# First loads in another order, and the statistics of the first chunk in two halves, in a layer norm + S5 + SwiGLU kernel

## The chip, the cores and the metric

The kernel runs on one core of one Trainium2 chip. The metric is the device time of one execution in microseconds; the median of three runs before the change is 200.81 us (200.62 to 201.2).

## The reference

One input x of 2048 tokens by 512 features (bf16) is normalised per token, and three things are added: x itself, a diagonal complex state-space layer (S5) on the normalised input, and a SwiGLU feed-forward block on it with 1792 hidden features.

```python
xn = _layernorm(x, axis=-1)                      # mean and variance over the 512 features
# S5: Bu = xn @ B_bar.T ; h[t] = Lam_bar * h[t-1] + Bu[t] ; y = 2 Re(h @ C.T) + xn * Dskip
# SwiGLU: out = (silu(xn @ w1) * (xn @ w3)) @ w2
return x + S5(xn) + SwiGLU(xn)
```

w1 and w3 are 512 x 1792, w2 is 1792 x 512.

## The kernel before

The 2048 tokens are taken in four blocks of 512; a block has four chunks of 128 tokens, one token to a partition. For each block the kernel normalises the chunks, brings the normalised block to the layout with features on partitions (`xnT`), multiplies it with w1 and w3 for the 14 hidden tiles of 128 (function `glu`), gates the results, projects to the state (`bu`), scans along time, and multiplies gates and states with w2 and C together (`y_fast`). The order of every engine's instructions is the order in which the Python program writes them, since the kernel schedules by hand; side tasks are put between by a small planner (`Filler`), which does not act before the first three hidden tiles are done.

The change touches the start alone, that is block 0 up to its third hidden tile. The names:

- Loads. `nc.sync.dma_start` issues on SP's queue, `nc.scalar.dma_start` on ACT's. Lines 164 to 170 are the first loads. x of block 0 comes by chunk: chunks 0 and 1 in two halves of 256 features each (128 x 256 bf16, 64 KB), one on SP and one on ACT; chunk 3 whole (128 KB) on ACT; chunk 2 whole on SP. Then `load_w` (line 155) loads columns 0 to 255 of w1 (line 156) and of w3 (line 157), and then columns 256 to 511 of both, 256 KB each, all on SP. Both weights bear the name `w_sb` in the profile.
- ACT's program begins with its three loads, then loads a table of functions (line 199). SP's holds loads alone.
- `bulk_loads` (line 172) issues the next stage on SP: columns 512 to 1023 of w1 and w3, block 1 of x, and transposing loads. Its first instruction is a small one on ACT that reads chunk 0's scale and writes into w1, so the loads do not go before that scale is known.
- TensorE begins with ten matmuls on constants (`keep_busy`, line 196).
- `ln_stats` (line 217) takes a chunk's mean and variance on VectorE: one `bn_stats` over 512 features (line 219) and one `bn_aggr` (line 220). `ln_first_rstd` makes the scale on ACT (lines 233 and 234). `ln_apply` (line 224) normalises on VectorE. `ln_first_transpose` transposes on TensorE (line 243) and copies out on ACT (line 244).
- `quarter(cl, fs)` (line 619) are the matmuls of one chunk's 128 tokens with hidden tiles `fs`: the w1 side first, then the w3 side. Tiles 0 and 1 use columns 0 to 255, tile 2 uses columns 256 to 383.
- After the first two quarters come the transposed parameters of S5 (line 315), chunk 2's transposes, tile 2 of chunk 0, chunk 3's transposes, and so on; the dense loop over the other hidden tiles is line 587.

On VectorE the order is: statistics of chunk 0, statistics of chunk 1, chunk 0 normalised in two halves, chunk 1 normalised, statistics of chunks 2 and 3, both normalised.

Of the kernel before, what the change touches and what calls it, by code (L numbers as in the profile page):

```python
# [14 lines left out]
FP32 = DT.float32  # L15
BF16 = DT.bfloat16
FP16 = DT.float16
P = 128
# [45 lines left out]
def kernel(  # L64
# [17 lines left out]
    nc = tc.nc  # L82
    _, S, D = A_x.shape
# [21 lines left out]
    D1, D2 = slice(0, DH), slice(DH, D)  # L105
# [3 lines left out]
    xv = A_x[0].rearrange("(c p) d -> p c d", p=P)  # L109
# [5 lines left out]
    lnp = ctx.enter_context(tc.tile_pool(name="lnp", bufs=2))  # L115
# [28 lines left out]
    mv_all = const.tile([P, NCH, 2], FP32, name="mv_all")  # L144
# [6 lines left out]
    x_blk = [x_all[:, i] for i in range(NBLK)]  # L151
# [3 lines left out]
    def load_w(f0, f1, eng1=nc.sync, eng3=nc.sync):  # L155
        eng1.dma_start(out=w1_sb[:, :, f0:f1], in_=w1v[:, :, f0:f1])
        eng3.dma_start(out=w3_sb[:, :, f0:f1], in_=w3v[:, :, f0:f1])
# [3 lines left out]
        for i in range(0, CPB, n):  # L161
            nc.sync.dma_start(out=x_blk[b][:, i:i + n, :], in_=xv[:, b * CPB + i:b * CPB + i + n, :])

    for c in range(2):
        for eng, dsl in ((nc.sync, slice(0, D // 2)), (nc.scalar, slice(D // 2, D))):
            eng.dma_start(out=x_blk[0][:, c, dsl], in_=xv[:, c, dsl])  # L166
    nc.scalar.dma_start(out=x_blk[0][:, 3, :], in_=xv[:, 3, :])
    nc.sync.dma_start(out=x_blk[0][:, 2, :], in_=xv[:, 2, :])
    load_w(0, 2 * P)
    load_w(2 * P, 4 * P)  # L170

    def bulk_loads():
        nc.scalar.activation(out=w1_sb[:, 0, 4 * P:4 * P + 1], in_=rstd_all[:, 0:1], func=ACT.Copy)
        load_w(4 * P, MID * P)
        load_x(1)
        nc.sync.dma_start_transpose(out=bt[:, 0], in_=A_B_re)
        nc.sync.dma_start_transpose(out=bt[:, 1], in_=A_B_im)
        load_w(MID * P, F)
        nc.sync.dma_start_transpose(out=ct_in[:, :, 0, :], in_=A_C_re)
        nc.sync.dma_start_transpose(out=ct_in[:, :, 1, :], in_=A_C_im)  # L180
# [13 lines left out]
    def keep_busy(n, cols):  # L194
        for _ in range(n):
            nc.tensor.matmul(out=wps[:, 0:cols], lhsT=ones[:, 0:P], rhs=ones[:, 0:cols], start=True, stop=True)
# [20 lines left out]
    def ln_stats(b, cl):  # L217
        stats = lnp.tile([P, 6], FP32, name="stats", bufs=4)
        nc.vector.bn_stats(out=stats, in_=x_blk[b][:, cl, :])
        nc.vector.bn_aggr(out=mv_all[:, b * CPB + cl, :], in_=stats)  # L220

    def ln_apply(b, cl, dsl=slice(0, D)):
        c = b * CPB + cl
        nc.vector.tensor_scalar(out=xn_blk[b][:, cl, dsl], in0=x_blk[b][:, cl, dsl], scalar1=mv_all[:, c, 0:1],
                                scalar2=rstd_all[:, c:c + 1], op0=ALU.subtract, op1=ALU.mult)
# [5 lines left out]
    def ln_first_rstd(cl):  # L231
        lnv = lnp.tile([P, 1], FP32, name="lnv")
        nc.scalar.activation(out=lnv, in_=mv_all[:, cl, 1:2], func=ACT.Ln, bias=eps_t, scale=1.0)
        nc.scalar.activation(out=rstd_all[:, cl:cl + 1], in_=lnv, func=ACT.Exp, scale=-0.5)

    def ln_first_transpose(cl, parts=1):
        n = NDT // parts
        for i in range(0, NDT, n):
            if parts > 1:
                ln_apply(0, cl, slice(i * P, (i + n) * P))  # L240
            pxt = ps_y.tile([P, n, P], BF16, name="y_ps")
            for k in range(n):
                nc.tensor.transpose(out=pxt[:, k, :], in_=xn_blk[0][:, cl, (i + k) * P:(i + k + 1) * P], identity=ident)
            nc.scalar.activation(out=xnT_blk[0][:, i:i + n, cl * P:(cl + 1) * P], in_=pxt, func=ACT.Copy)
# [68 lines left out]
    def params_transpose():  # L313
        pps = ps_y.tile([P, NP3], BF16, name="y_ps")
        nc.tensor.transpose(out=pps, in_=par_rows, identity=ident[0:NP3, 0:NP3])
        return pps

    def params_dt(pps):
        nc.scalar.activation(out=par, in_=pps, func=ACT.Copy)
        nc.scalar.activation(out=dtv, in_=par[:, 0:NPT], func=ACT.Exp)  # L320
        gp.tensor_tensor(out=kr, in0=dtv, in1=lre, op=ALU.mult)

    def params_turn():
        gp.tensor_tensor(out=turn, in0=dtv, in1=lim, op=ALU.mult)
        gp.tensor_scalar(out=turn, in0=turn, scalar1=1.0 / TWO_PI, scalar2=None, op0=ALU.mult)
        gp.tensor_scalar(out=fr, in0=turn, scalar1=MAGIC, scalar2=None, op0=ALU.add)
        gp.tensor_scalar(out=fr, in0=fr, scalar1=-MAGIC, scalar2=None, op0=ALU.add)
        gp.tensor_tensor(out=fr, in0=turn, in1=fr, op=ALU.subtract)
        gp.tensor_scalar(out=t0, in0=turn, scalar1=0.25, scalar2=None, op0=ALU.add)
        gp.tensor_scalar(out=ab, in0=t0, scalar1=MAGIC, scalar2=None, op0=ALU.add)  # L330
        gp.tensor_scalar(out=ab, in0=ab, scalar1=-MAGIC, scalar2=None, op0=ALU.add)
        gp.tensor_tensor(out=ab, in0=t0, in1=ab, op=ALU.subtract)
        gp.tensor_tensor(out=den, in0=lre, in1=lre, op=ALU.mult)
        gp.tensor_tensor(out=t0, in0=lim, in1=lim, op=ALU.mult)
        gp.tensor_tensor(out=den, in0=den, in1=t0, op=ALU.add)
# [245 lines left out]
    def glu(b):  # L581
# [10 lines left out]
        def evac(f, g_ps, u_ps):  # L592
            if f % 2 == 0:
                pair[:] = [glup.tile([P, 2, TBLK], BF16, name="g16"), glup.tile([P, 2, TBLK], BF16, name="u16")]
            g16, u16 = pair
            nc.scalar.activation(out=g16[:, f % 2, :], in_=g_ps, func=ACT.Silu)  # L596
            nc.scalar.activation(out=u16[:, f % 2, :], in_=u_ps, func=ACT.Copy)  # L597
            if f % 2 == 1:
                pend.append((f, g16, u16))

        def gate():
            f, g16, u16 = pend.pop(0)
            bg.own(0.6, -0.5)
            nc.vector.tensor_tensor(out=act_gates(b, f - 1), in0=split(g16), in1=split(u16), op=ALU.mult)  # L604
# [3 lines left out]
        if b == 0:  # L608
            f0 = FIRST
            tiles = first_ps  # L610

            def quarter(cl, fs, parts=1):
                tsl = slice(cl * P, (cl + 1) * P)
                n = NDT // parts
                for side, w in ((0, w1_sb), (1, w3_sb)):
                    for i in range(0, NDT, n):
                        for f in fs:
                            for dt in range(i, i + n):
                                nc.tensor.matmul(out=tiles[2 * f + side][:, tsl], lhsT=w[:, dt, f * P:(f + 1) * P],  # L619
                                                 rhs=xnT[:, dt, tsl], start=(dt == 0), stop=(dt == NDT - 1))  # L620

            ln_stats(0, 0)
            ln_first_rstd(0)
            bulk_loads()
            ln_stats(0, 1)
            ln_first_rstd(1)
            ln_first_transpose(0, 2)
            keep_busy(4, P)
            ln_apply(0, 1)
            ln_first_transpose(1)  # L630
            ln_stats(0, 2)
            ln_first_rstd(2)
            ln_stats(0, 3)
            ln_first_rstd(3)
            ln_apply(0, 2)
            ln_apply(0, 3)
            quarter(0, (0, 1), 2)
            quarter(1, (0, 1))
            pps = params_transpose()
            params_dt(pps)  # L640
            params_turn()
            table_angles(0, 2)
            ln_first_transpose(2)
            quarter(0, (2,))
            ln_first_transpose(3)
            quarter(1, (2,))
            nc.scalar.activation(out=rho, in_=kr, func=ACT.Exp)
            nc.scalar.preload_act_table_set("silu_and_others")
            quarter(2, range(FIRST))
            for f in range(FIRST):  # L650
                quarter(3, (f,))
            evac(0, tiles[0], tiles[1])
            evac(1, tiles[2], tiles[3])
            evac(2, tiles[4], tiles[5])
            gate()
            bg.tensor(0.0)
            bg.fill()
# [516 lines left out]
    bg.add(0.0, late_loads, ("ln", 1))  # L1174
    bg.add(0.2, params_w)
    gate = glu(0)
    bg.flush(("ln", 1))
    gate()
# [36 lines left out]

    ssm_tasks(1, between=[(0.2, lambda: keep_ends(0))])
    gate = glu(1)
    gate()
    bg.flush(("sums", 0))
# [8 lines left out]
    ssm_tasks(2, between=res_list(3), late=[(0.2, lambda: keep_ends(1)), *row_sums(2, *pairs[2]), *column_sums(3)])  # L1228
    bg.first(bu_sums(2))
    gate = glu(2)  # L1230
    gate()
    sin_step(("norm", 3, CPB - 1))
# [50 lines left out]
```

## Time and profile before

| what | value |
|---|---|
| median of three runs | 200.81 us |
| the profiled execution: its time from the first to the last instruction (span) | 199.5 us |
| TensorE busy in the span | 195.6 us (98%) |
| VectorE busy | 181.8 us (91%) |
| ACT busy | 135.0 us (68%) |
| POOL busy | 51.5 us (26%) |
| granted TensorE clock, mean | 0.999 |

The profile is one execution on the chip; its times count from the start of the span. PE is TensorE's matmuls, PEld its weight loads, DVE is VectorE, and SPq and ACTq are the issuing of loads on these two queues. A line such as "L619 PE MATMUL gu_ps<-xnT,w_sb ... x8" is a group of eight instructions of line 619 that write gu_ps from xnT and w_sb, and a bracket at its end says how long the engine was idle before it and what ended that. The chain is the work that ended last, followed back from the end; in its pieces each stands with start and length. The execution's own time is told as its span; the medians are of whole runs and some 1.3 us longer.

### The profile page before, as it was taken

The page shows a single profiled execution, that of the slowest core. Times are in us where ns is not written, and L with a number is a line of the kernel's source. Part 1 is how long each engine was busy: PE and PEld are TensorE (multiplying, and loading weights), DVE is VectorE, ACT ScalarE, POOL GpSimd, SP SyncE. Part 2 cuts the span into 40 slices and gives each one's busy share as a digit, 9 for nine tenths or more (in the row PEclk, how much of TensorE's full clock was granted, in tenths as well). Part 3 has the DMA queues.
Part 4 walks back from the last instruction along what each step waited for, and adds up shares of the span by engine and source line. Part 5 has one row for each costly group of instructions (what it writes and reads, how often), then busy time and mean ns, then how long its engine had stood idle before and what let it go on. Part 6 is the DMA issues. An engine that isn't in the chain of part 4 may idle for free.

```text
span 199.5 us, 3700 instructions
## 1 busy us (share of the span) xinstructions
PE 195.6 (98%) x1401; PEld 130.7 (65%) x1401; DVE 181.8 (91%) x254; ACT 135.0 (68%) x281; POOL 51.5 (26%) x75
## 2 busy tenths in 40 slices
PE   8999999999999999999999999999999999999994
PEld 2774444444444488866555468888566678888893
DVE  3689699999999999989999997999999999999972
ACT  4699897699999996968998684362588783111220
POOL 7180289700411134041202305040021303310000
PEclk9999999999999999999999999999999999999999
DMA  4999996991497054730997455838137732941111
GB/s 138 326 277 200 302 186 124 343 273 23 69 181 141 0 105 82 135 105 0 156 148 119 89 92 98 172 83 132 53 59 129 149 56 52 174 92 36 53 44 40
DMA packets 32258, 25.12 MB, mean 126 GB/s; under 512 B 16240, under 2 KB 29936, under 8 KB 32240
## 3 DMA queue, kind: packets, MB, share of 16 engines
q0 software_dynamic: 6128, 11.38, 33.5%
q1 hardware_dynamic: 25536, 13.21, 26.8%
q10 hardware_dynamic: 576, 0.30, 0.5%
q8 instruction: 11, 0.18, 0.4%
q14 instruction: 7, 0.06, 0.1%
HBM read 7.74 MB, written 2.10 MB: 49 GB/s over the span
## 4 chain that ended last, share of the span: by engine, by line
PE 95%; DMA 2%; SPq 1%; issue 0%; DVE 0%
PE gu_ps L587 34%; PE gu_ps L1054 17%; PE y_ps L1054 10%; PE gu_ps L848 7%; PE bu_ps L1054 7%; PE bu_ps L454 3%; PE y_ps L454 3%; PE y_ps L869 3%; PE y_ps L780 3%; DMA w_sb<-in_B_w_dram 2%; PE gu_ps L619 2%; PE gu_ps L780 2%; PE bu_ps L869 1%; PE bu_ps L780 1%; PE bu_ps L619 1%; SPq L166 0%
## 5 line engine op out<-in xcount | busy, mean ns | idle before, releaser
L587 PE MATMUL gu_ps<-xnT,w_sb 128*128 128x512 bf16 x312 | 69.6, 379 | 0.0
L587 PEld LDWEIGHTS <-w_sb 128*128 128x128 bf16 x312 | 30.5, 98 | 34.2
L1054 PEld LDWEIGHTS <-act 128*128 128x128 f16 x462 | 43.5, 98 | 5.4
L596 ACT ACTIVATE g<-gu_ps 128x512 bf16<-128x512 f32 x41 | 24.8, 606 | 6.0 <-PE gu_ps L587 3.6
L597 ACT ACTIVATE u<-gu_ps 128x512 bf16<-128x512 f32 x41 | 24.8, 606 | 4.5 <-PE gu_ps L587 3.7
L505 DVE TENSOR_TENSOR_SCAN u<-rho,ends,u 128x512 bf16<-128x512 f32 x16 | 20.0, 1270 | 0.0
L527 POOL DMA_DIRECT2D act<-p x7 | 9.2, 1320 | 34.0 <-DVE act L519 22.1
L1054 PE MATMUL gu_ps<-w_sb,act 128*128 128x256 bf16 (+3 forms) x126 | 16.0, 267 | 0.0
L848 PE MATMUL gu_ps<-xnT,w_sb 128*128 128x512 bf16 x64 | 15.9, 379 | 0.0
L604 DVE TENSOR_TENSOR act<-g,u 128x1024 f16<-128x1024 bf16 x21 | 14.2, 679 | 0.4 <-ACT u L597 0.4
L860 ACT ACTIVATE g<-gu_ps 128x512 bf16<-128x512 f32 x14 | 8.4, 599 | 5.4 <-PE gu_ps L848 5.0
L454 PEld LDWEIGHTS <-bt 128*128 128x128 bf16 x64 | 6.3, 98 | 7.5
L1077 ACT ACTIVATE x_blk<-gu_ps 128x256 f32<-128x256 f32 (+1 forms) x9 | 3.3, 368 | 10.6 <-PE gu_ps L1054 10.6
L1054 PE MATMUL bu_ps<-w_sb,act 128*128 128x256 bf16 (+3 forms) x84 | 10.4, 264 | 0.0
L1054 PE MATMUL gu_ps<-ct,act 128*128 128x256 f16 (+1 forms) x72 | 10.4, 267 | 0.0
L848 PEld LDWEIGHTS <-w_sb 128*128 128x128 bf16 x64 | 6.3, 98 | 4.8
L505 DVE TENSOR_TENSOR_SCAN u<-rho,u 128x512 bf16<-128x512 f32 x8 | 9.2, 1206 | 0.0
L1054 PEld LDWEIGHTS <-x_blk 128*128 128x128 f16 x88 | 8.6, 98 | 1.0
L1054 PEld LDWEIGHTS <-tw 128*128 128x128 f16 x88 | 8.6, 98 | 1.0
L513 DVE TENSOR_TENSOR p<-u,tabe 128x2048 f16<-128x2048 bf16 (+1 forms) x8 | 8.7, 1085 | 0.1
L519 DVE TENSOR_TENSOR act<-u,tabe 128x2048 f16<-128x2048 bf16 (+1 forms) x8 | 8.7, 1083 | 0.0
L488 DVE TENSOR_TENSOR u<-u,tabe 128x2048 bf16<-128x2048 bf16 x7 | 8.5, 1219 | 0.1
(203 smaller groups left out, 392.5 us busy)
## 6 DMA issues: line engine op xcount, KB each, us to landing
act<-p POOLq DMA_DIRECT2D x6, 512.0 KB, 6.1
xn<-x_blk POOLq DMA_DIRECT2D x4, 512.0 KB, 5.5
out_dram<-xn SPq DMA_DIRECT2D x15, 128.0 KB, 1.7
w_sb<-in_B_w_dram SPq DMA_DIRECT2D x1, 1792.0 KB, 8.2
act<-act POOLq DMA_DIRECT2D x5, 352.0 KB, 4.6
w_sb<-in_B_w_dram SPq DMA_DIRECT2D x2, 768.0 KB, 6.4
u<-p POOLq DMA_DIRECT2D x3, 512.0 KB, 5.1
w_sb<-in_B_w_dram SPq DMA_DIRECT2D x4, 256.0 KB, 4.9
```

The lines of the kernel that those rows point to most:

```text
L454: nc.tensor.matmul(out=ps, lhsT=bt[:, ri, dt, pt * P:(pt + 1) * P], rhs=xnT_blk[b][:, dt, :], start=(dt == 0), stop=(dt == NDT - 1))
L505: nc.vector.tensor_tensor_scan(out=v, data0=rho[:, pt:pt + 1].to_broadcast([P, TBLK]), data1=v, initial=init, op0=ALU.mult, op1=ALU.add)
L513: nc.vector.tensor_tensor(out=by_state(st["p16"][:, csl]), in0=by_chunk(st["g"][:, :, ::-1, tsl]), in1=by_chunk(tabe[:, psl, 2:0:-1, tsl]) ...
L519: nc.vector.tensor_tensor(out=by_state(act_state(b, hf)[:, csl]), in0=by_chunk(st["g"][:, :, :, tsl]), in1=by_chunk(tabe[:, psl, 0:1, tsl] ...
L527: gp.dma_start(out=a, in_=p16, accum_op=ALU.add)
L587: nc.tensor.matmul(out=ps[:, tsl], lhsT=w[:, dt, f * P:(f + 1) * P], rhs=xnT[:, dt, tsl], start=(dt == 0), stop=(dt == NDT - 1))
L596: nc.scalar.activation(out=g16[:, f % 2, :], in_=g_ps, func=ACT.Silu)
L597: nc.scalar.activation(out=u16[:, f % 2, :], in_=u_ps, func=ACT.Copy)
L604: nc.vector.tensor_tensor(out=act_gates(b, f - 1), in0=split(g16), in1=split(u16), op=ALU.mult)
L780: nc.tensor.matmul(out=out[:, h * TH:(h + 1) * TH], lhsT=left[:, h, k, :], rhs=right[:, k, :], start=(start and h == 0 and k == 0), stop=( ...
L848: nc.tensor.matmul(out=ps, lhsT=w[:, dt, f * P:(f + 1) * P], rhs=xnT[:, dt, :], start=(dt == 0), stop=(dt == NDT - 1))
L1054: nc.tensor.matmul(out=out, lhsT=left[:, k, :], rhs=right[k][:, cols], start=(start and k == 0), stop=(k == NK - 1), skip_group_check=True)
```

## The change

Two edits, both in the start of block 0.

The first loads are issued in another order. Chunk 0 still comes as two halves, one on SP and one on ACT. Chunk 1 comes whole on ACT, second in that queue. Columns 0 to 255 of w1 come second on SP, and those of w3 third on ACT. Chunks 2 and 3 follow on SP, and then columns 256 to 511 of w1 and w3, also on SP.

Chunk 0's statistics are taken by two `bn_stats`, one over each half of the features, into one tile of two groups, and one `bn_aggr` over both groups. The other chunks keep `ln_stats`.

```diff
-    for c in range(2):
-        for eng, dsl in ((nc.sync, slice(0, D // 2)), (nc.scalar, slice(D // 2, D))):
-            eng.dma_start(out=x_blk[0][:, c, dsl], in_=xv[:, c, dsl])
-    nc.scalar.dma_start(out=x_blk[0][:, 3, :], in_=xv[:, 3, :])
-    nc.sync.dma_start(out=x_blk[0][:, 2, :], in_=xv[:, 2, :])
-    load_w(0, 2 * P)
+    def load_chunk(c, eng, dsl=slice(0, D)):
+        eng.dma_start(out=x_blk[0][:, c, dsl], in_=xv[:, c, dsl])
+
+    load_chunk(0, nc.sync, D1)
+    load_chunk(0, nc.scalar, D2)
+    load_chunk(1, nc.scalar)
+    load_w(0, 2 * P, nc.sync, nc.scalar)
+    load_chunk(2, nc.sync)
+    load_chunk(3, nc.sync)
     load_w(2 * P, 4 * P)
...
-            ln_stats(0, 0)
+            stats = lnp.tile([P, 2, 6], FP32, name="stats2", bufs=1)
+            for h, dsl in enumerate((D1, D2)):
+                nc.vector.bn_stats(out=stats[:, h, :], in_=x_blk[0][:, 0, dsl])
+            nc.vector.bn_aggr(out=mv_all[:, 0, :], in_=stats.rearrange("p h s -> p (h s)"))
             ln_first_rstd(0)
```

D1 and D2 are the slices of features 0 to 255 and 256 to 511; `load_w(f0, f1, eng1, eng3)` takes the queue of w1 and that of w3.

## The prediction

> **What bounds the kernel now.** I read the page's chain first (what set the end), then its first pieces in order of time, then the waits of the first microseconds, then the first transfers with their landing times, and last the rate of the transfers by stretch.
>
> ```profile
> PE 95%; DMA 2%; SPq 1%; issue 0%; DVE 0%
> ```
>
> The end is set by TensorE from the first matmuls on: nothing waits between there and the last store, so whatever moves TensorE's start of gap-free work moves the end by as much. The 2% (4.5 us) of transfer in the chain is the start. Its first pieces (start, length, what):
>
> ```profile
> 2.58 4.53 DMA w_sb<-in_B_w_dram
> 7.11 0.05 issue
> 7.16 1.51 PE gu_ps L619 x24
> 8.67 0.11 PE y_ps L315
> 8.78 0.33 PE y_ps L243 x4
> 9.11 0.58 PE bu_ps L619 x8
> 9.69 0.22 PE y_ps L243 x4
> 9.92 0.45 PE bu_ps L619 x8
> ```
>
> The transfer that ends last is w3's first quarter (columns 0 to 255), issued at 2.58 and landed at 7.11. Behind it TensorE has no gap but one that hides in a length: eight matmuls take 0.45 us at 9.92 and 0.58 at 9.11. The 0.13 more is a wait inside that group. The group uses w1 and w3 columns 256 to 383, and that w3 load, issued at 3.69, lands 5.6 later, at 9.29, where the group's second half begins. So there are two late weights, not one. The waits of 4 to 10 us name the first:
>
> ```profile
> PEld L619 <- DMA w_sb<-in_B_w_dram: 0.6, 2, 0.4
> PE gu_ps L619 <- DMA w_sb<-in_B_w_dram: 0.3, 1, 0.3
> PE y_ps L243 <- DVE xn L224: 0.2, 1, 0.2
> ```
>
> What leads up to it on VectorE, and TensorE beside it:
>
> ```profile
> 3.08 0.69 DVE L219 BATCH_NORM_STATS2 stats<-x_blk 128x6 f32<-128x512 bf16 x1 [3.08 <-DMA x_blk<-in_A_x_dram]
> 3.90 0.67 DVE L219 BATCH_NORM_STATS2 stats<-x_blk 128x6 f32<-128x512 bf16 x1
> 4.71 1.09 DVE L224 TENSOR_SCALAR xn<-x_blk,mv_all,rstd_all 128x256 bf16<-128x256 bf16 x3
> 5.86 0.40 PE L243 MATMUL y_ps<-ident,xn 128*128 128x128 bf16 x4
> 6.27 0.62 PE L619 MATMUL gu_ps<-xnT,w_sb 128*128 128x128 bf16 x8
> ```
>
> VectorE takes both statistics in a row, then normalises. Chunk 1's statistics (3.90) stand ahead of chunk 0's normalising (4.71) in its queue. TensorE's transposes of chunk 1 end at 6.26. The first transfers (issue kind, KB, us from issue to landing), in the order c2, c3, then w1 and w3 columns 0 to 255, then w1 and w3 columns 256 to 511:
>
> ```profile
> x_blk<-in_A_x_dram SPq DMA_DIRECT2D x1, 128.0 KB, 3.7
> x_blk<-in_A_x_dram ACTq DMA_DIRECT2D x1, 128.0 KB, 4.0
> ...
> w_sb<-in_B_w_dram SPq DMA_DIRECT2D x1, 256.0 KB, 4.1
> ...
> w_sb<-in_B_w_dram SPq DMA_DIRECT2D x1, 256.0 KB, 4.5
> ...
> w_sb<-in_B_w_dram SPq DMA_DIRECT2D x1, 256.0 KB, 5.2
> ...
> w_sb<-in_B_w_dram SPq DMA_DIRECT2D x1, 256.0 KB, 5.6
> ```
>
> The halves of chunks 0 and 1 took 2.1 (SP) and 2.3 to 2.4 (ACT). The rate by stretch (engines' busy time, then granted clock, DMA share, GB/s):
>
> ```profile
> 2.00:2.80 0.80, 0.80 (x3) 0.29 (x2) 0.00 (x0) 0.67 (x1) 0.80 (x3) 1.00 1.22 300
> 2.80:4.40 1.60, 1.60 (x5) 0.59 (x4) 1.29 (x3) 0.91 (x2) 1.53 (x3) 1.00 0.57 167
> 5.20:9.20 4.00, 3.71 (x53) 2.90 (x51) 2.79 (x8) 2.65 (x11) 0.00 (x0) 1.00 1.14 322
> ```
>
> From 2.8 to 4.4 the transfers run at half the rate of before and after. I do not know why; it weighs on every step below.
>
> **The change part by part.**
>
> *What could be gained at most.* With both first weights there when chunk 1's transposes end (6.26), the 32 matmuls of the first two quarters take 4 x 0.45 = 1.80 and end at 8.06 instead of 8.67: 0.61. With the second w3 load in time too, 0.58 becomes 0.45: 0.13 more. In all 0.74, less any shift S of chunk 1's transposes. The clock costs nothing: it is granted at 1.00 in these stretches.
>
> *Issues.* SP had seven loads ahead of the next stage, issued at 0.73, 1.17, 1.64, 2.11, 2.58, 3.13 and 3.69; it now has six: c0's half, w1, c2, c3, second w1, second w3. w1 goes 2.11 to 1.17, c2 stays at 1.64, c3 goes from ACT's 1.65 to SP's 2.11, the second w1 3.13 to 2.58, the second w3 3.69 to 3.13. ACT still issues three (c0's half, c1 whole at 1.17, w3 at 1.65 instead of 2.58), so its table load stays at 2.13, done at 3.41, with 0.68 of idle behind it. The next stage's loads wait for chunk 0's scale and are issued at 4.88 as before; SP is free earlier, which costs and gives nothing. POOL's three parameter loads are not passed by anything.
>
> *Statistics of chunk 0.* One operation of 0.69 becomes two over 256 columns, still one aggregation (0.18). The nearest row for a halved operation is the normalising one: 0.41 for 512 columns, 0.31 for 256, so 0.21 of it is fixed; taken so, a half of the statistics costs about (0.69 + 0.21) / 2 = 0.45. SP's half lands at 2.83, ACT's at 3.02 to 3.06: the first runs 2.85 to 3.30, the second to 3.75, against 3.77 now. From -0.2 (halves without a fixed part) to +0.2 (both wait for the later half); I take 0.
>
> *Chunk 1.* It now lands as one 128 KB load on ACT's queue at 1.17, beside w1 on SP's. Bounds: as its halves did, 1.17 + 2.1 = 3.3, and as c3 did, 1.17 + 4.0 = 5.17. By bytes: c0's 131 KB is through by about 2.4. Then c1 and as much of w1, 262 KB, go together: 120 KB to 2.8 at 300 GB/s, 142 KB at 167 GB/s, to 3.65. Chunk 0's halves landed some 0.5 after their last bytes, so chunk 1 lands at about 4.15. Its slot is that of the halves and its size that of c3; the value lies between. Its statistics start at 4.15 instead of 3.90: S = +0.25. Behind that wait on VectorE stand chunk 0's normalising, and so the first transposes, and everything to 7.75. Gain left: 0.74 - 0.25 = 0.49.
>
> *Chunks 2 and 3.* They are now behind w1 on SP. c3 lands between 2.11 + 4.1 = 6.2 and 2.11 + 5.2 = 7.3; by bytes as much is ahead of it as was ahead of the end of the first w3 (7.11), so about 6.8. From chunk 3's statistics (6.54 now) to chunk 2 normalised (7.75) are 1.21: 8.0. TensorE would want it at 8.71 - 0.49 = 8.22. Covered by 0.2; at 7.3 the cover is gone and TensorE starts chunk 2's transposes at about 8.6, gain 0.1.
>
> *The second w3.* Once the first weights are early, this load is late next. Bounds: 9.29 as now (the same 1.57 MB go ahead of it and with it), and 3.13 + 5.2 = 8.33 by the row of the load that had its slot. Weights now stand in both queues while the transfers ran half empty; of the (300 - 167) x 1.6 = 0.21 MB lost there I give back half, 0.1 MB at 322 GB/s, 0.33, and round it to a landing at 8.9. Gain left: 9.29 - 8.9 = 0.39.
>
> The Trainium skill (DMA: Bandwidth & Descriptors, "Issuing engines are not separate DMA queues") speaks against this change: loads issued from several engines run on the same 16 DMA engines, and spreading them saves only the issuing time. By that rule the second w3 would land as now and the sum would be 0. The stretch at a share of 0.57 says that the engines were not full then, so more loads in the queues may still use them; no run here shows it yet.
>
> *Sum.* The smallest of 0.49, 0.39 and what chunks 2 and 3 allow, so about 0.36 after rounding for their joint risk. The profiled execution's span goes from 199.5 to about 199.1; it lies 1.3 under the median of the runs, 200.81, and I carry that over: 200.45. A change of 0.3% (0.6 us) is about what a measurement of this kernel can tell from none, so this is no change by that bound.
>
> **The rivals.**
>
> *All three are early (faster).* If chunk 1 lands by 3.9 (c1's halves landed at 3.3 to 3.57, which speaks for it) and the second w3 by 8.5 (its slot's row gives 8.33), the whole 0.74 comes, 0.84 if the halved statistics give 0.1: 200.0 to 200.1. Against it: both want the slow stretch of 2.8 to 4.4 to be an effect of the old order.
>
> *The second w3 lands as now.* Then TensorE stops for it at 9.29 with all else done: gain 0 to 0.05, 200.8. For it: 322 GB/s from 5.2 on, hardly more than that to win.
>
> *Chunk 1 late (slower).* If w1 takes the transfer engines and chunk 1 waits behind it, VectorE stands with chunk 0's finished statistics. The gain is 0.74 - (T - 3.90) for a landing at T: nothing at T = 4.64, 0.6 lost at T = 5.24. c3's row gives 5.17 and 201.3; the first w3's latency, 4.5, gives T = 5.67 and a loss of 1.03, 201.85. For it: both 128 KB rows, 3.7 and 4.0, against 2.1 to 2.4 for 64 KB. Against it: they ran in the slow stretch, chunk 1 would start before it.
>
> **How the numbers follow.** Partial gain, 200.2 to 200.8, likeliest value 200.45: 0.40. Second w3 as now: 0.08. All early: 0.30. Chunk 1 late enough to cost over 0.6: 0.22. Faster 0.30, same 0.40 + 0.08 = 0.48, slower 0.22. The range reaches to 199.95, which takes in nearly all of the fast case, and to 201.35 (c3's row), which leaves out two thirds of the slow one: about 0.83 inside.
>
> **What the profile after would show.** Right: no wait of L619 on the first weights; chunk 1's statistics with a wait on its load, starting near 4.15; eight matmuls on the second weights some 0.4 earlier but still longer than 0.45. Wrong on chunk 1: its statistics at 3.8, or past 4.6. Wrong on the transfers: the half-rate stretch gone, or the second w3 at 9.3. Wrong on chunks 2 and 3: transposes at 8.2 waiting for VectorE. The whole sum is wrong if a gap opens on TensorE after 13 us, where none is now.

## The result, and the profile after

The changed kernel takes 201.77 us (median of 11 runs, 201.38 to 203.12), the kernel before 200.92 (median of 11 runs beside it, 200.62 to 201.59). The ratio is 1.0047 with an interval of 1.0031 to 1.0063: slower by 0.3 to 0.6%. The prediction was 200.45, range 199.95 to 201.35. Single runs that a disturbance of the chip lengthened by a tenth or more are left out here and below.

The profiled execution of the changed kernel has a span of 199.6 us, hardly more than the 199.5 of the first profile of before, and its own time is 201.42. So a run's time lies 1.8 above its span, not 1.3 as the prediction took it. The first profile of before is therefore one of about 201.3, at the long end of its kind, and the profile after is one of the shorter ones of its own.

The chain of the changed kernel as a whole, and its first pieces in order of time (start, length, what; lines have moved by 3: L222 and L227 are the statistics and the normalising, L246 the transposes, L622 the first quarters, L199 matmuls on constants):

```profile
PE 95%; DMA 2%; DVE 1%; issue 0%; ACTq 0%
```

```profile
1.15 3.52 DMA x_blk<-in_A_x_dram
4.67 0.02 issue
4.69 0.71 DVE stats L222
...
5.89 0.54 PE y_ps L246 x4
6.43 0.23 PE bu_ps L199 x4
...
6.67 0.40 PE y_ps L246 x4
7.07 1.79 PE gu_ps L622 x32
8.86 0.11 PE y_ps L318
...
9.29 0.45 PE bu_ps L622 x8
```

The 2% of transfer is no longer a weight but chunk 1 of x: issued at 1.15, landed at 4.67. The weights have done what they were moved for: the 32 matmuls of the first two quarters run without a gap (1.79), and the group on the second weights takes 0.45 instead of 0.58. All of it starts later, since the statistics of chunk 1 start at 4.69, and chunk 0's normalising stands behind them. The waits of 4 to 10 us:

```profile
PE y_ps L246 <- DVE xn L227: 1.3, 1, 1.3
...
DVE stats L222 <- DMA x_blk<-in_A_x_dram: 0.7, 1, 0.7
```

The two stretches of the transfers that tell why (after the busy times: granted clock, DMA share, GB/s):

```profile
2.40:3.20 0.80, 0.80 (x3) 0.30 (x2) 0.22 (x1) 0.80 (x1) 0.80 (x2) 1.00 0.41 101
3.20:4.40 1.20, 1.20 (x5) 0.40 (x3) 0.74 (x3) 0.60 (x2) 1.13 (x3) 1.00 1.10 354
```

The same two stretches in the first profile of before:

```profile
2.40:3.20 0.80, 0.80 (x3) 0.29 (x2) 0.12 (x1) 0.80 (x1) 0.80 (x2) 1.00 1.09 242
3.20:4.40 1.20, 1.20 (x4) 0.44 (x3) 1.17 (x3) 0.51 (x2) 1.13 (x3) 1.00 0.54 170
```

The slow stretch is still there, but at 2.4 to 3.2, straight behind chunk 0's halves and ahead of chunk 1. In the first profile of before it began near 2.8, when about as many bytes had moved as chunks 0 and 1 hold together (an estimate from the rates): there chunk 1 was nearly through when it began.

### The profile page after: what moved, and what is told of

It reads as the page before. It is cut to its first block, busy times and chain, and to the rows that moved or that the text cites. A ratio compares the mean times of both kernels' runs of the same rounds, so it can differ in the third digit from the quotient of the medians.

```text
span 199.6 us, 3685 instructions
## 1 busy us (share of the span) xinstructions
PE 194.1 (97%) x1388; PEld 130.7 (65%) x1401; DVE 182.0 (91%) x255; ACT 135.0 (68%) x281; POOL 51.8 (26%) x75
## 4 chain that ended last, share of the span: by engine, by line
PE 95%; DMA 2%; DVE 1%; issue 0%; ACTq 0%
PE gu_ps L590 34%; PE gu_ps L1060 17%; PE y_ps L1060 10%; PE gu_ps L854 7%; PE bu_ps L1060 7%; PE bu_ps L457 3%; PE y_ps L457 3%; PE y_ps L875 3%; PE y_ps L786 3%; PE gu_ps L622 2%; DMA x_blk<-in_A_x_dram 2%; PE gu_ps L786 2%; PE bu_ps L875 1%; PE bu_ps L786 1%; PE bu_ps L622 1%; PE y_ps L246 1%
## 5 line engine op out<-in xcount | busy, mean ns | idle before, releaser
L590 PE MATMUL gu_ps<-xnT,w_sb 128*128 128x512 bf16 x304 | 68.9, 379 | 0.4
L854 PE MATMUL gu_ps<-xnT,w_sb 128*128 128x512 bf16 x61 | 15.6, 379 | 0.1
```

Source lines behind the costliest of these rows:

```text
L590: nc.tensor.matmul(out=ps[:, tsl], lhsT=w[:, dt, f * P:(f + 1) * P], rhs=xnT[:, dt, tsl], start=(dt == 0), stop=(dt == NDT - 1))
L854: nc.tensor.matmul(out=ps, lhsT=w[:, dt, f * P:(f + 1) * P], rhs=xnT[:, dt, :], start=(dt == 0), stop=(dt == NDT - 1))
```

## The experiments

Theory A: chunk 1's late load costs the time. Theory B: the first profile of before was not typical. Theory C: TensorE's gap ahead of the transposes costs clock in some runs. Theory D: the split statistics cost.

**The kernel before, again.** No edit.

> The kernel before, unchanged, for a second profiled execution. Theory A (the change is judged against an execution like the first profile): TensorE again waits some 0.6 us in all for the first weights, span 199.5. Theory B (the first profile of before was a slow one of its kind, since a time of 201.4 goes with a span of 199.6 in the changed kernel, while the median of before is 200.9): the weights land earlier than 6.2 and 7.1 in a typical execution, the waits of L619 are under 0.3 us in all, and the span is about 199.0. Time ratio 1.000 either way.

Ratio 0.9998 (0.9988 to 1.0008), 10 runs of 200.67 to 201.53. Span of the profiled execution 199.1. Its chain:

```profile
2.60 4.23 DMA w_sb<-in_B_w_dram
6.84 0.05 issue
6.88 1.51 PE gu_ps L619 x24
...
8.83 0.45 PE bu_ps L619 x8
```

The first w3 lands at 6.83 instead of 7.11, and the second weights are no wait (0.45). The first two quarters end at 8.40; without any wait they would have ended at 8.08. So this execution offers 0.32 for earlier weights, not 0.74. Its own time is 200.89, a little under the median of its batch (201.04), as the first one, of about 201.3, is over it; a middle execution lies between the two. Theory B holds: the span is 199.1 (about 199.0 was expected), TensorE's matmuls wait 0.2 on the weights, and w3 lands before 7.1.

**The changed kernel, again.** No edit.

> The changed kernel, unchanged, for a second profiled execution and more times. Its runs spread from 201.38 to 203.12, those of before from 200.62 to 201.59. Theory A (chunk 1's landing varies): where the span is longer than 199.6, chunk 1's statistics start later than 4.69 by as much. Theory C (TensorE's clock): chunk 1 starts at about 4.7 in every execution, and a longer span shows matmuls at 0.43 us per 512 columns after 5.9. Ratio 1.004 to 1.006.

Ratio 1.004 (1.002 to 1.006). Span 200.0; chunk 1's statistics at 5.01, the 32 matmuls in 1.79. By theory A the span is longer by 0.4 and the statistics later by 0.3. The profiled run is one of the shorter ones, so it does not test theory C. Of the 11 runs two are at 202.95 and 203.29 and nine at 201.33 to 201.79, nothing between.

**The order of the loads alone.**

```diff
-            stats = lnp.tile([P, 2, 6], FP32, name="stats2", bufs=1)
...
-            nc.vector.bn_aggr(out=mv_all[:, 0, :], in_=stats.rearrange("p h s -> p (h s)"))
+            ln_stats(0, 0)
```

> The new order of the loads alone, chunk 0's statistics as one operation. Theory A (chunk 1's whole load beside w1 is the cause): ratio 1.004 to 1.006 as in the whole change, chunk 1's statistics start at about 4.7. Theory D (the split statistics cost): ratio under 1.002.

Ratio 1.0047 (1.0025 to 1.007), chunk 1's statistics at 4.63, four of 12 runs at 202.88 to 203.32. The order alone gives the whole loss, as far as these intervals tell.

**The split statistics alone.** The loads of before with the second edit of the change.

> The split statistics alone, loads as before. Theory A: ratio 0.999 to 1.001; the first aggregation ends within 0.1 us of 3.99. Theory D: ratio 1.003 or more.

Ratio 0.9996 (0.9982 to 1.0009). VectorE of this kernel:

```profile
2.82 0.75 DVE L624 BATCH_NORM_STATS2 stats<-x_blk 128x6 f32<-128x256 bf16 x2 [2.82 <-DMA x_blk<-in_A_x_dram]
3.61 0.21 DVE L625 BATCH_NORM_AGGREGATE mv_all<-stats 128x2 f32<-128x12 f32 x1
```

Two halves take 0.75 against 0.69 for the whole, start as soon as the first half is there, and the aggregation ends at 3.82 instead of 3.99, 0.17 earlier, a little more than the 0.1 given. It is not seen in the time, whose interval is wider than that. Theory D falls.

**Chunk 1 again in two halves, ahead of the weights.**

```diff
-    load_chunk(1, nc.scalar)
+    load_chunk(1, nc.sync, D1)
+    load_chunk(1, nc.scalar, D2)
```

> The changed kernel with chunk 1 again in two halves, one on each queue, ahead of the first weights; w1 then follows on SP and w3 on ACT, chunks 2 and 3 behind w1. Theory A (chunk 1 is late because it is one load whose data go through after those of w1 begin): its statistics follow chunk 0's without a wait, near 3.9, TensorE starts near 5.1, the long gap on TensorE is gone and with it the runs near 203; ratio 0.997 to 0.999. If chunks 2 and 3 behind w1 are a cause of their own: TensorE waits for VectorE at 8 to 9 us, ratio over 1.000.

Ratio 0.9999 (0.9987 to 1.0011). Chunk 1's statistics start at 3.90 and no run is near 203, as theory A has it, and the loss is gone. But the gain did not come. VectorE and the waits of TensorE from 4 to 10 us in this kernel:

```profile
6.68 0.69 DVE L223 BATCH_NORM_STATS2 stats<-x_blk 128x6 f32<-128x512 bf16 x1 [0.90 <-DMA x_blk<-in_A_x_dram]
```

```profile
PE y_ps L247 <- DVE xn L228: 0.3, 1, 0.3
```

Chunk 2, behind w1 as in the changed kernel, lands at 6.66, and TensorE waits 0.3 for it until 8.74. The second expectation holds in its mechanism; its ratio over 1.000 does not, and neither does theory A's of 0.997 to 0.999.

**Chunk 2 ahead of w1 on SP.** Chunk 1 stays one load of 128 KB, second on ACT; its neighbour on SP is now chunk 2.

```diff
-    load_w(0, 2 * P, nc.sync, nc.scalar)
     load_chunk(2, nc.sync)
+    load_w(0, 2 * P, nc.sync, nc.scalar)
```

> The changed kernel with chunk 2 second on SP and w1 third: chunk 1 is still one 128 KB load second on ACT, but its neighbour on SP is chunk 2, of its own size, not w1. If the neighbour w1 delays chunk 1: its statistics start before 4.2. If the size of chunk 1's load does: they start at 4.6 or later as in the changed kernel. Ratio 0.998 to 1.001 in the first case, 1.003 to 1.006 in the second.

Ratio 0.9998 (0.9984 to 1.0012). VectorE, and the two stretches of the transfers:

```profile
3.77 0.21 DVE L628 BATCH_NORM_AGGREGATE mv_all<-stats 128x2 f32<-128x12 f32 x1
3.90 0.64 DVE L222 BATCH_NORM_STATS2 stats<-x_blk 128x6 f32<-128x512 bf16 x1
```

```profile
2.40:3.20 0.80, 0.80 (x3) 0.29 (x2) 0.22 (x1) 0.80 (x1) 0.80 (x2) 1.00 0.94 313
3.20:4.40 1.20, 1.20 (x5) 0.34 (x3) 1.17 (x4) 0.49 (x2) 1.13 (x3) 1.00 0.67 177
```

Chunk 1 whole is in time without a wait. The size of its load is not the cause; w1's load second on SP is. What of w1's load does it (its size of 256 KB, its layout) is not told apart. w1 is issued at 1.67 here instead of 1.19, and the slow stretch moves from between 2.4 and 3.2 to behind 3.2. No run is as long as 202.8; the highest is 202.02. The loss is gone here too, and again nothing is gained: TensorE waits for the first weights until 6.38.

**Twelve matmuls on constants in the changed kernel.**

```diff
-    NWARM = 10
+    NWARM = 12
```

> The changed kernel with 12 instead of 10 matmuls on constants at the start, so that TensorE's gap of 1.3 us ahead of the first transposes shrinks to 0.9 or less. Chunk 1 lands as late as before the edit. In 34 runs of the new order 9 took 202.87 or more, and 21 runs without it none. Theory C (in those runs the gap keeps the clock at half rate for another stretch, some 1.5 us lost): none or one run of 12 over 202.6, median 201.4 to 201.6. Theory A alone (the long runs are late landings of chunk 1): three of 12 over 202.6 as before.

Ratio 1.0027 (1.0013 to 1.004), median 201.73; chunk 1's statistics at 5.12 in its profile, the gap on TensorE 0.28. No run of 11 is at 202.6 or more; the highest is 202.24. As theory C expected, except for the median; if a quarter of the runs were long as before, none of 11 would come about once in 24 times. What is left, 0.27% or 0.54 us (0.26 to 0.8 by the interval), is the price of the late chunk less what the earlier weights give back.

**Seven matmuls on constants in the kernel before.** `NWARM = 7`.

> The kernel before with 7 instead of 10 matmuls on constants, so that TensorE idles from 3.8 to 5.1, a gap like that of the changed kernel, with the loads as before. Theory C: about a quarter of the runs 1 to 2 us longer, the others as before (200.6 to 201.6). Theory A alone: all runs as before.

Ratio 1.0055 (1.0034 to 1.0076): all six runs at 201.84 to 202.72, not a quarter of them. The 32 matmuls take 2.71 in the chain. Matmuls at half rate cost time here with the loads as before, but this kernel both has a gap (1.22) and does less ahead of it, and the two are not told apart.

**Eight in the changed kernel.** `NWARM = 8`.

> The changed kernel with 8 matmuls on constants instead of 10, so that TensorE's gap ahead of the first transposes grows from 1.3 to about 2.1 us, with chunk 1 as late as in the changed kernel. Theory C: more than half of the runs at 202.6 to 203.6 and in such a profile the first 32 matmuls of L622 take 2.7 to 3.4 us instead of 1.8. Theory A alone: runs as in the changed kernel, a quarter or fewer over 202.6, the 32 matmuls in 1.8.

Ratio 1.0071 (1.0045 to 1.0097). Seven of ten runs are at 202.38 to 203.46, three at 201.33 to 201.46. TensorE in the profiled one, a run of 202.38:

```profile
5.84 0.65 PE L246 MATMUL y_ps<-ident,xn 128*128 128x128 bf16 x4 [1.51 <-DVE xn L227]
...
7.14 2.68 PE L622 MATMUL gu_ps<-xnT,w_sb 128*128 128x128 bf16 x32
```

Chunk 1's statistics start at 4.64, no later than elsewhere; the matmuls are what is long: 2.68 against 1.95 in the same view of the changed kernel, just under the 2.7 expected. The gap is 1.51, not 2.1. Most runs are long, as theory C has it; but here too fewer matmuls and a longer gap come together.

**w3 on ACT, all of x ahead of all weights.** The split statistics with the x loads of before, and `load_w(0, 2 * P, nc.sync, nc.scalar)`.

> The old order of the x loads and the split statistics, with one thing of the change more: w3's first columns go fourth on ACT's queue, behind chunk 3, instead of fifth on SP's. Every x load stands ahead of every weight in its own queue. The issue takes 0.45 to 0.53 us more of ACT ahead of its table load (2.1 to 2.6, done at 3.9 against a first use at 4.1). If the wait of 0.2 us for w3 that a typical execution of before shows is the issue's lateness: no wait of L619, span 0.2 shorter, ratio about 0.999. If it is the transfer engines' rate: ratio 1.000.

Ratio 0.9994 (0.9982 to 1.0006). The wait for w3 is not gone. In the waits of 4 to 10 us it stands with the weight loads:

```profile
PEld L619 <- DMA w_sb<-in_B_w_dram: 0.2, 1, 0.2
```

In the second profile of before it is 0.3 there. A gain cannot be told from nothing. None of these orders beats the kernel before clearly.

**The changed kernel, six more profiles of one run each.** No edit; the last two have the expectation of the one ahead of them.

> The changed kernel again, for one more profiled execution. If it is one of the long ones (202.8 or more): Theory C expects chunk 1's statistics at 4.6 to 5.1 as in the others and the first 32 matmuls of L622 in over 2.4 us; theory A alone expects the statistics past 6 and the 32 matmuls in 1.8. If it is a short one (201.3 to 202): 32 matmuls in 1.8 and statistics at 4.6 to 5.1 by both.

> As the run before: the changed kernel again, for one more profiled execution, with the same two expectations for a long one and the same for a short one.

> The changed kernel again. If it is a long one (202.8 or more), theory C expects chunk 1's statistics at 4.6 to 5.1, the transposes of chunk 0 0.65 us and the first 32 matmuls of L622 2.4 us or more; theory A alone expects the statistics past 6 and the 32 matmuls in 1.8. If it is short, both expect 4.6 to 5.1 and 1.8.

> The changed kernel on one more execution: if long, half-rate matmuls by theory C, late statistics by theory A alone.

The times were 201.31, 201.61, 201.62, 203.28, 201.39 and 201.56; chunk 1's statistics started at 4.59, 4.79, 4.80, 4.79, 4.66 and 4.84. The long one, the fourth, had chunk 1 at the same time as the one before it. The chain of the run of 201.62, span 199.8:

```profile
1.16 3.62 DMA x_blk<-in_A_x_dram
4.78 0.02 issue
4.80 0.70 DVE stats L222
...
6.00 0.54 PE y_ps L246 x4
6.54 0.23 PE bu_ps L199 x4
...
7.18 1.79 PE gu_ps L622 x32
```

and that of the run of 203.28, span 201.4:

```profile
1.16 3.60 DMA x_blk<-in_A_x_dram
4.76 0.02 issue
4.79 0.70 DVE stats L222
...
5.98 0.65 PE y_ps L246 x4
6.63 0.43 PE bu_ps L199 x4
...
7.49 3.13 PE gu_ps L622 x32
```

Up to 6 us the two chains are the same. Then the four constant matmuls take 0.43 instead of 0.23 and the 32 of the quarters 3.13 instead of 1.79: half rate for most of them, 1.6 us of span. So a long run is one with matmuls at half rate, not one with a later chunk 1: theory A alone falls for the long runs and stands for the others. That the late chunk 1 brings the long runs is shown by the counts: behind the same ten constant matmuls 10 of 40 runs are long with chunk 1 late, and none of 23 in the two orders that have it in time (chunk 1 in two halves, chunk 2 ahead of w1).

## Why the prediction was wrong

Two terms of its sum were mis-sized, chunk 1's landing (4.15 us; 4.67 in the first profile after) and the gain it is set against (0.74; 0.32 in the second profile of before), and the clock, which it put at nothing, costs some 0.4 on average.

**The sum.** In the typical executions chunk 1's statistics start at 4.79 (middle of eight profiles of the changed kernel, 4.59 to 5.01) instead of 3.92. That is S = 0.87, of which the earlier weights give back 0.32 by the second profile of before: 0.55. The runs that are not long lie 0.63, 0.47 and 0.40 above the kernel before in the first three batches of the new order, and the run with twelve constant matmuls measures 0.54. Besides, 10 of 40 runs of the new order with ten constant matmuls were long (202.87 or more, the others at most 202.02), and the pair shown above puts a long one 1.6 above a short one: 0.4 on average. Together 0.95, against 0.0047 x 201 = 0.94 measured. The interval of that is 0.62 to 1.27, so an agreement to 0.01 is luck.

**Chunk 1's landing: the term that was mis-sized.** The step took 4.15, from bytes over the rates of the old stretches: 300 GB/s to 2.8 and 167 after. It measured 4.67 in the first profile, and the start of the statistics at 4.69 is past the 4.6 that the prediction itself named as its sign of being wrong here. The rates were those of the old order, taken as if they were tied to the time in the trace; with w1 second on SP the slow stretch began 0.4 earlier (near 2.4 instead of 2.8), at 101 GB/s and ahead of chunk 1. The formula for the loss itself held: it gave a loss of 0.05 for a start at 4.69 against the first profile of before, and the spans were 199.6 and 199.5.

**The most that could be gained.** 0.61 + 0.13 were right for the execution that was read and too much for a middle one: 0.32 in the second one. The trace is one execution, and the offset of 1.3 to the median hid that it was a long one. Even at 4.15 the change would, by that second profile, have won nothing but 0.32 - 0.23 = 0.09.

**"The clock costs nothing."** This was wrong. The prediction moved the first transposes by S and priced the shift alone; that TensorE then stands idle before its full rate is settled it put at nothing, because the granted clock read 1.00. The range fails even without this: its upper end is 201.35, and the shortest of the eleven runs takes 201.38. The rival of a late chunk 1 named the right mechanism and place; its threshold for a loss of 0.6, T = 5.24, was put too far out, since both the gain was smaller than 0.74 and the clock was left out.

**What held.** The split statistics cost nothing that can be seen. Chunks 2 and 3 were covered (no wait of TensorE for them in the profile after), and only because everything was late: with chunk 1 in time chunk 2 becomes the wait. The second w3 was to land at 8.9; issued at 3.15 it took 5.1, 8.25, earlier than thought. How much of that is the change's is not known, since the second profile of before has no wait for it either. ACT's table load moved by 0.09 alone and cost nothing.

## What to carry to other kernels

A load that feeds the head of the chain can be held up by a large load issued beside it on another queue. Here the 256 KB of w1 one slot later on SP (issued at 1.67 instead of 1.19) left chunk 1 in time; beside it, what was gained on the weights (0.32) was paid more than twice on the chunk ahead of them (0.87). Before a gain of half a per cent is taken from one profile, see where that execution lies in the spread of the runs, and take a second one if it can be had. In this kernel a wait at the start costs, in some runs, more than its length, since it opens a gap on TensorE while full rate is not settled yet; price the matmuls behind it at both rates.

## What was not expected of the hardware

The clock at the start. The constant matmuls start 0.43 us apart at first and 0.22 apart once the full rate is up, and the moment of that differs from run to run of one program: the ten take 3.82 to 4.43 us in nine profiles of the new order. In five of them the rate rose before the gap and stayed up through a gap of 0.71 to 1.32. In the four others all ten ran at half rate, and the gap was 0.67 to 0.85; three came out of it at full rate, and one, the long one, had half rate for the next 4 us and more. These are TensorE's first matmuls and first transposes in the last of the six profiles, a run of 201.56, and then in the long one:

```profile
0.76 4.43 PE L199 MATMUL bu_ps<-const-bfloat16-1.0 128*128 128x512 bf16 x10 [0.76 <-PEq L1273]
6.04 0.54 PE L246 MATMUL y_ps<-ident,xn 128*128 128x128 bf16 x4 [0.85 <-DVE xn L227]
```

```profile
0.76 4.43 PE L199 MATMUL bu_ps<-const-bfloat16-1.0 128*128 128x512 bf16 x10 [0.76 <-PEq L1273]
5.98 0.65 PE L246 MATMUL y_ps<-ident,xn 128*128 128x128 bf16 x4 [0.80 <-DVE xn L227]
```

So the length of the gap alone does not decide. No run of the kernel before, whose gap is 0.16 in its first profile, was as long; the highest is 201.81. The granted clock in the profile does not show it. This is the stretch of the long run with the half-rate matmuls, and it reads 1.00:

```profile
5.90:8.50 2.60, 2.52 (x24) 2.39 (x25) 2.24 (x7) 1.93 (x8) 0.00 (x0) 1.00 1.16 309
```

The duration of a group shows it: 32 matmuls of 128 columns in 1.79 or in up to 3.13. The Trainium skill (TensorE: Matmul & The Clock Gate, "What's actually happening") tells of a window of about 3.4 us that runs freely and is not reset by the kernel, and of full rate only after a busy one. The runs agree in kind: the same program has two lengths 1.6 us apart, and two constant matmuls more or fewer change how often. They do not give the moment: with chunk 2 ahead of w1 the ten constants take 3.63, so the rate rose less than 3 us after the first matmul; with w3 on ACT it rose only some 5 us after it, with no gap between. That a gap inside one such window is the exact condition is argued, not shown.

The slow stretch of the transfers. From 2.4 to 3.2 the transfers move 81 to 155 GB/s in the eleven profiles with w1 second on SP, and 183 to 313 in the seven others: w1 in that slot brings the slow stretch ahead of chunk 1. Elsewhere it does not simply follow w1's issue. It comes 1.2 us after it in the changed kernel (issue 1.19), 1.5 where chunk 2 stands ahead of w1 (1.67) and 0.7 in the first profile of before (2.11); and in the second profile of before, with the same order as the first, it was weaker (276 GB/s from 3.2 to 4.4, against 170). What it is, and why it varies from run to run, stays open.
